# Second LayerNorm of three MLP chunks: turned rows kept and scaled instead of turned again

## The chip, the cores and the metric

The kernel runs on one core of a Trainium2 chip. A core has five engines that work side by side, each through its own list of instructions in order: PE (matrix products and transposes through the matrix unit, results into PSUM), ACT (functions of one input, element by element), DVE (element-wise work and reductions), POOL (element-wise work on SBUF) and SP (issues DMAs). They wait for each other through semaphores. The metric is the time of one execution on the device, in microseconds (us); lower is better.

## The reference

One block in which attention and an MLP run side by side on the same normalized input, for S = 2048 tokens of width D = 448, all in float32:

```python
xn = _layernorm(x, axis=-1)
out = x + A(xn) + B(xn)
# A: 16 heads of 28, one K and one V for all heads, softmax over 2048 keys
# B: y = _layernorm(xn); h = gelu(y @ w1 + b1)   (448 -> 1792);   h @ w2 + b2
```

The MLP normalizes a second time: `_layernorm(m) = (m - mean) / sqrt(var + 1e-5)` of rows that are already normalized. Their mean is zero but for rounding, so the second LayerNorm is one factor per token.

## The kernel before, in words

Tokens are handled in NCH = 4 chunks of CW = 512 (CT = 4 tiles of 128). A product in float32 is made of three products of two halves each: a high part and the rest, `xh` and `xl`, with the same split of the weights (`w1h`, `w1l`, `w2h`, `w2l`). For the products the normalized rows must stand turned, the 448 channels on partitions in four blocks b, the 512 tokens of a chunk along the row. The fourth block has 64 channels, which stand twice.

**Before the MLP** (lines 442 to 477). For each chunk four slots project Q, K and V from `xts[c, False]` (`q_slot`, line 352); beside them the next chunk is normalized and turned. That is `norm_parts` (line 249): `center` (line 255) scales and shifts a tile of 128 tokens on ACT and, for 64 channels, on DVE; `turn` (line 268) makes four transposes on PE into one PSUM bank, ACT copies the high part into `xh`, DVE subtracts it from the bank into `xl`. `xh` and `xl` are rings of two tiles. The evacuation of a Q slot writes `qe` and two stores of it to DRAM (`qd`, line 377); that of the first slot of a chunk also writes K: `kl` (line 372) and three copies into `ks` (line 374), all on SP's queue. SP also loads the weights here (lines 100 to 102 and 334), and POOL splits w1 (`w1_split`, line 325), whose buffers are then loaded again. The fourth group of slots turns chunk 0 for the second LayerNorm, with `lnq` and `lnqb` as factor and shift.

**The MLP** (lines 584 to 707) is 56 slots, chunk by chunk, 14 slots a chunk. PE's order is written out by hand: slot n runs `mlp1` of (c, ft), 11 matmuls into the one bank `ph`, and then `mlp2` of slot n - 2, 12 matmuls into four banks that gather over a chunk. Between them stand, nine to a slot, score tiles of the attention: L521 (a maximum over keys is reduced from it on DVE, L522) and L555 (kept, through DVE, and later exponentiated on ACT, L573, and stored to `td` by SP, L576). Both use the pool `mp`, three banks named m. ACT reads `ph` twice (`hx` L603, `hz` L604); POOL works out the inside of the GELU (L605, L606), ACT the tanh (L609), POOL the rest (L610, L611); in the next slot ACT makes `hh` (L616) and POOL `hl` (L618), which `mlp2` reads one slot later. `mlp2` has twelve places, `stages` 0 to 11, behind whose matmuls these pieces are issued. In chunk 0 each odd slot also splits a part of w2 (L342 on ACT, L346 on DVE and POOL).

The second LayerNorm of chunks 1 to 3 stands in slots 5, 7, 9, 11 and 13 of the chunk before (line 677): `norm_gen` (line 303) gets x again, four line loads of 224 KB (`line`, line 245), centers a tile at stage 8 and turns the one before at stage 4, through the bank `ph`. In these slots `texp` (the exps) stands at stages 5 and 6 rather than 0 and 1.

**After the MLP** come the scores, the exps and the products with V for all heads; they read what the earlier stages left in SBUF and DRAM, and are not touched.

SP, like every engine, issues in the order of the program. A DMA waits there for what it reads, for its buffer, and for the one eight DMAs earlier.

Of the kernel before, what the change touches and what calls it, by code (L numbers as in the profile page):

```python
# [19 lines left out]
CT = 4  # L20
# [11 lines left out]
RAWS = 2  # L32
GELU = 0.044715, 0.7978845608028654
LEAD = 11
NH = 8
HD = D // 2

# [2 lines left out]
def block_kernel(ctx, tc, x, wq, wk, wv, wo, w1, b1, w2, b2, out):  # L40
# [8 lines left out]
    mpx = ExitStack()  # L49
    mp = mpx.enter_context(tc.tile_pool(name="mp", bufs=3, space=PSUM))  # L50
    dram = ctx.enter_context(tc.tile_pool(name="dram", bufs=1, space=bass.MemoryType.DRAM))
    xt_p = ctx.enter_context(tc.tile_pool(name="xt", bufs=2))
    qmp = ctx.enter_context(tc.tile_pool(name="qmp", bufs=1))

    def heads_of(u):
# [5 lines left out]
    ld = dram.tile([4, CW], F32, name="ld")  # L61
    ad = dram.tile([P, NT, D], F32, name="ad")
    td = {u: dram.tile([32, 4, 4 * CT, 512], F32, name=f"td{u}") for u in TURNED}
    qd = [dram.tile([D, S], F32, name=f"qd{i}") for i in range(2)]

    ks = keep.tile([P, S], F32R, name="ks")
# [1 line left out]
    ident = keep.tile([P, P], F32, name="ident")  # L68

    ph1 = ExitStack()  # L70
    xl_p = ph1.enter_context(tc.tile_pool(name="xl", bufs=2))
# [5 lines left out]
    lnqb = wp.tile([P, NT], F32, name="lnqb")  # L77
    b1t = wp.tile([P, NF], F32, name="b1t")
    b1s = wp.tile([P, NF], F32, name="b1s")
    b2b = wp.tile([P, D], F32, name="b2b")  # L80
# [52 lines left out]
    make_identity(nc, ident)  # L133
    one = keep.tile([P, 1], F32, name="one")
    warm = keep.tile([P, 1], F32, name="warm")
    pool.memset(one, 1.0)
    pool.memset(f(wah[:, :, 0:64]), 0.0)
    pool.memset(f(wal[:, :, 0:64]), 0.0)
# [92 lines left out]
    def norm_both():  # L231
        dve.tensor_mul(lnq, lnp[:, :, 1], lnr)
        dve.tensor_mul(lnq, lnq, lnr)
        r = rstd(lnq, lnq, NT)
        next(r)
        yield
        next(r)
        dve.tensor_mul(lnq, lnq, lnr)
        dve.scalar_tensor_tensor(lnqb, lnp[:, :, 0], -1.0, lnq, op0=ALU.mult, op1=ALU.mult)
        act.activation(warm, one, AF.Tanh)  # L240
        yield
# [3 lines left out]
    def line(t):  # L245
        lines[t] = keep.tile([P, D], F32, name="a", bufs=4)
        nc.sync.dma_start(lines[t], xv[:, t, :])

    def norm_parts(c, second, first=False, bank=mtile):
        xh = xt_p.tile([P, 4, CW], F32R, name="xh")  # L250
        xl = xl_p.tile([P, 4, CW], F32R, name="xl")
        xts[c, second] = xh, xl
        xns = {}

        def center(k):
            t = CT * c + k
            if first:
                xn = f(wqp.tile([P, 2, CW], F32R, name="qe", bufs=5))[:, 0, :]
            else:
                xn = tmp.tile([P, 4 * P], F32, name="xn", bufs=2)  # L260
            scale, bias = (lnq, lnqb) if second else (lnr, lnb)
            src = lines.pop(t) if second and c else xin[t]
# [3 lines left out]
            xns[k] = xn  # L266

        def turn(k):
            sl = slice(k * P, (k + 1) * P)
            pt = bank([P, 4, P])  # L270
            for b in range(4):
                pe.transpose(pt[:, b, :], xns[k][:, b * P:(b + 1) * P], ident)
            act.activation(xh[:, :, sl], pt, AF.Copy)
            dve.tensor_sub(xl[:, :, sl], pt, f(xh[:, :, sl]))

        return center, turn
# [23 lines left out]
        turn(3)  # L300
        next(first)

    def norm_gen(c, bank):
        center, turn = norm_parts(c, True, False, bank)
        for k in range(CT + 1):
            if k > 0:
                turn(k - 1)
            yield
            if k < CT:
                center(k)  # L310
            yield

    wl_q = []

# [131 lines left out]
    for c in range(NCH):  # L446
        center, turn = norm_parts((c + 1) % NCH, c + 1 == NCH, bank=lambda shape: (qbank, mtile)[next(turns) % 2](shape))
        for i in range(4):
            ev = q_slot(c, i)
            if vt is not None:  # L450
                v_slot(c, vt)
                vt = None
            if evac is not None:
                vt = evac()
            evac = ev
            if i in ((2, 3) if c == 0 else (1, 3)):
                n = 2 * c + i // 3
                w1_split(n)
                if n < 2:
                    w1_load(n + 4)  # L460
                elif n == 3:
                    w1_load2(6)
                elif n in (4, 5):
                    w2_load(n - 4)
                if n in (2, 3):
                    qms.append(load_m(*heads[n - 2]))
                elif n in (4, 5):
                    load_m(TURNED[n - 4], 3, q3[n - 4])
            for job in more.get((c, i, True), ()):
                job()  # L470
            for part, k in (("", "c0 c1", "t0 c2 t1 c3", "t2 t3") if c == 0 else
                            ("c0 c1", "t0 c2 t1 c3", "t2 t3", ""))[i].split():
                (center if part == "c" else turn)(int(k))
            for job in more.get((c, i, False), ()):
                job()
    evac()
# [2 lines left out]
    def load_q(u, blocks=range(4)):  # L479
        c, g = units[u]  # L480
        cols = slice(c * CW, (c + 1) * CW)
        if u < 2 and 0 in blocks:
            qst.append(xt_p.tile([P, 4, CW], F32R, name="xh"))
# [138 lines left out]
    def mlp2(c, ft, stages):  # L622
        if ft == 0:
            m2s[c] = [m2p.tile([P, CW], F32, name=f"m2_{k}")[:, 0:D] for k in range(CT)]
        m2 = m2s[c]
        hh, hl = hs.pop((c, ft))
        terms = ((hh, w2h), (hh, w2l), (hl, w2h))
        order = [(k, i) for k in range(CT) for i in range(3)]
        if (c, ft) == (0, 0):
            order.sort(key=lambda e: e[1])  # L630
        for n, (k, i) in enumerate(order):
            h, w = terms[i]
            pe.matmul(m2[k], h[:, k * P:(k + 1) * P], w[:, ft, :], start=(ft == 0 and i == 0),  # L633
                      stop=(ft == NF - 1 and i == 2))
            if ft == NF - 1 and i == 2:
                t = CT * c + k
                a = lines.pop(t)
                dve.tensor_add(a, a, m2[k])
                nc.sync.dma_start(ad[:, t, :], a)
            stages[n]()  # L640
            yield

    def slot(n):
        nonlocal maxed, ending, later_low
        middle = high = low = none
        closing, ending = ending, none
        if n < len(mslots):
            if split(*mslots[n]):
                high, low = w2_split(n // 2)
                if n > 1:  # L650
                    high()
            middle, ending = yield from mlp1(*mslots[n])
# [16 lines left out]
    def none():  # L669
        pass  # L670

    norms, maxed, ending, later_low = {}, 0, none, none
    mslots = [(c, ft) for c in range(NCH) for ft in range(NF)]
    for c in range(1, NCH):
        g = norm_gen(c, lambda shape: php.tile(shape, F32, name="ph"))
        for i in range(CT + 1):
            norms[NF * (c - 1) + 5 + 2 * i] = lambda g=g: next(g, None)
    mxs.add(max_stream())
    done = 0
    for n in range(len(mslots) + 2):  # L680
        c, ft = mslots[n] if n < len(mslots) else (NCH, n - len(mslots))
        if 3 <= ft < 11 and ft % 2 and c < NCH - 1:
            line(CT * (c + 1) + (ft - 3) // 2)
        if 9 < ft:
            line(CT * c + ft - 10)
            if ft > 10:
                a = lines[CT * c + ft - 11]
                pool.tensor_add(a, a, b2b)
        if ft == 0 and n:
            a = lines[CT * c - 1]  # L690
            pool.tensor_add(a, a, b2b)
        if (c, ft) == (NCH - 1, 8):
            load_q(0)
# [260 lines left out]
```

## Time and profile before

| | us |
|---|---|
| median of 3 runs | 1092.79 |
| lowest and highest | 1092.52, 1094.23 |
| the profiled execution | 1092.67 |
| its span on the core | 1090.9 |
| PE, DVE, ACT, POOL busy in it | 1079.5, 910.4, 736.4, 562.5 |

The granted clock of PE was 0.999 over the span. In a row of the timeline stand the start, the time taken, the engine, the line, the operation and its tiles (`out<-in`), and in brackets the engine's idle time before it and what ended that. A row of a line's answer has the lowest, median and highest duration in ns, and the first and last start. The rows of the stretches have the busy time of each engine, the granted clock, the share of time in which the 16 DMA engines were busy, and GB/s. PEld is PE's load of weights, SPq an issue on SP's queue.

### The profile page before, as it was taken

Reading aid. Unit: us, or ns where it says so; the run is one execution under the profiler, and the core shown is the slowest. Engines: PE = TensorE matmul, PEld = TensorE weight load, DVE = VectorE, ACT = ScalarE, POOL = GpSimd, SP = SyncE. Lnnn points to the kernel's source line nnn. Section 1 sums busy time; section 2 is a strip of 40 time slices with the busy share of each in tenths; the row PEclk is TensorE's granted clock in tenths of the full one; section 3 lists DMA queues with packets and bytes.
Section 4 is the critical chain, followed back from the end, with each engine's and each line's share of the span. In section 5 each row is a group of like instructions: output and inputs, shape, how many; then the busy total and the mean of one; then the engine's idle time right before and its main releaser. Section 6 shows DMA issues by size and latency. Waiting matters only on the chain.

```text
span 1090.9 us, 17542 instructions
## 1 busy us (share of the span) xinstructions
PE 1079.5 (99%) x5777; PEld 713.7 (65%) x5777; DVE 910.4 (83%) x1847; ACT 736.4 (68%) x1279; POOL 562.5 (52%) x694
## 2 busy tenths in 40 slices
PE   9999999999999999999999999999999999999998
PEld 8778888888888888865555556555556455555444
DVE  7789889888988998887898997899986889876744
ACT  6675565666666666559777776677775777765783
POOL 6359787778767877854343433433342343243220
PEclk9999999999999999999999999999999999999999
DMA  8774555777877777767977799588797778895720
GB/s 274 214 231 136 154 145 157 194 176 185 217 181 180 183 201 180 214 161 156 200 189 175 183 212 214 141 198 193 183 202 183 175 172 194 203 197 137 183 46 35
DMA packets 140512, 195.15 MB, mean 179 GB/s; under 512 B 17086, under 2 KB 96116, under 8 KB 140420
## 3 DMA queue, kind: packets, MB, share of 16 engines
q1 hardware_dynamic: 127684, 172.11, 63.0%
q0 software_dynamic: 11328, 21.33, 8.9%
q8 instruction: 46, 0.75, 0.3%
q10 hardware_dynamic: 1408, 0.57, 0.2%
q14 instruction: 46, 0.38, 0.1%
HBM read 115.22 MB, written 77.71 MB: 177 GB/s over the span
## 4 chain that ended last, share of the span: by engine, by line
PE 89%; ACT 3%; DVE 3%; DMA 2%; POOL 1%; issue 1%; SPq 0%; DVEq 0%; ACTq 0%; POOLq 0%
PE po L840 22%; PE m L521 17%; PE m L871 17%; PE m L633 10%; PE ph L180 9%; PE m L555 5%; PE qp L180 1%; DMA td<-raw 1%; PE m L752 1%; DVE mx L522 1%; PE m L753 1%; PE m L754 1%; PE ph L185 1%; PE ph L183 1%; ACT raw L573 1%; PE m L399 1%
## 5 line engine op out<-in xcount | busy, mean ns | idle before, releaser
L522 DVE TENSOR_REDUCE mx<-m 128x1 f32<-128x512 f32 x784 | 506.5, 680 | 81.1 <-PE m L521 72.3
L872 ACT ACTIVATE p<-m 128x512 f32<-128x512 f32 x784 | 402.6, 609 | 163.2 <-PE m L871 163.2
L521 PE MATMUL m<-ks,qm 128*128 128x512 f32 x784 | 322.1, 411 | 0.1
L871 PE MATMUL m<-xh,ks 128*128 128x512 f32 x784 | 258.6, 399 | 1.0 <-DVE half L723 1.0
L840 PE MATMUL po<-p,vs 128*32 128x512 f32 x2048 | 246.0, 598 | 0.0
L521 PEld LDWEIGHTS m<-ks,qm 128*128 128x128 f32 x784 | 147.0, 187 | 117.9 <-ACT p L872 34.5
L871 PEld LDWEIGHTS m<-xh,ks 128*128 128x128 f32 x784 | 144.2, 188 | 52.0 <-ACT p L872 15.0
L556 DVE TENSOR_SCALAR_CACHE_REDUCE raw<-m 128x512 f32<-128x512 f32 x240 | 161.1, 689 | 15.2 <-PE m L555 7.0
L854 DVE STREAM_TRANSPOSE p<-half 128x1024 f32<-128x1024 f32 x120 | 148.2, 1236 | 5.3 <-PE po L840 3.3
L573 ACT ACTIVATE raw<-raw,m 128x1024 f32<-128x1024 f32 x120 | 133.1, 1151 | 0.0
L840 PEld LDWEIGHTS po<-p,vs 128*32 128x32 f32 x2048 | 53.5, 109 | 120.1 <-issue 114.2
L603 ACT ACTIVATE hx<-ph,b1t 128x512 f32<-128x512 f32 x55 | 37.9, 690 | 131.9 <-PE ph L185 122.1
L555 PE MATMUL m<-ks,q 128*128 128x512 f32 x240 | 94.8, 395 | 1.1 <-DVE mx L522 0.6
L618 POOL TENSOR_TENSOR hl<-hx,hh 128x512 fp32r<-128x512 f32 x56 | 73.2, 1306 | 34.6 <-ACT hh L616 34.6
L633 PE MATMUL m<-w2h,hl 128*128 128x448 f32 x224 | 82.5, 370 | 0.3 <-POOL hl L618 0.3
L633 PE MATMUL m<-w2l,hh 128*128 128x448 f32 x224 | 81.4, 365 | 0.4 <-DVE w2l L346 0.4
L633 PE MATMUL m<-w2h,hh 128*128 128x448 f32 x224 | 81.4, 364 | 0.1
L611 POOL TENSOR_TENSOR hx<-hx,hz 128x512 f32<-128x512 f32 x56 | 73.1, 1306 | 4.7
L606 POOL TENSOR_TENSOR hz<-hz,hx 128x512 f32<-128x512 f32 x56 | 72.8, 1299 | 4.7
L508 POOL DMA_DIRECT2D xh<-mn x15 | 8.1, 543 | 124.3 <-ACT mn L504 124.3
L180 PE MATMUL ph<-xh,w1h 128*128 128x512 f32 x165 | 65.0, 394 | 0.0
L180 PE MATMUL ph<-xh,w1l 128*128 128x512 f32 x165 | 64.6, 391 | 0.0
(181 smaller groups left out, 1376.0 us busy)
## 6 DMA issues: line engine op xcount, KB each, us to landing
td<-raw SPq DMA_DIRECT2D x240, 256.0 KB
half<-td SPq DMA_DIRECT2D x120, 512.0 KB
xh<-qd POOLq DMA_DIRECT2D x60, 168.0 KB, 4.6
a<-in_A_x_dram SPq DMA_DIRECT2D x32, 224.0 KB
qm<-qd POOLq DMA_DIRECT2D x112, 56.0 KB, 4.4
qd<-qe SPq DMA_DIRECT2D x24, 256.0 KB
qm<-qd SPq DMA_DIRECT2D x84, 56.0 KB
ad<-a SPq DMA_DIRECT2D x16, 224.0 KB
```

What stands on the lines that cost most here:

```text
L180: pe.matmul(ps, w, v, start=(n == 0), stop=False)
L521: pe.matmul(pm, qm[:, t * P:(t + 1) * P], ks[:, n * CW:(n + 1) * CW], start=True, stop=True)
L522: dve.tensor_reduce(mx[:, CT * j + t, n:n + 1], pm, axis=AX.X, op=ALU.max)
L555: pe.matmul(sc, q3[i][:, t * P:(t + 1) * P], ks[:, n * CW:(n + 1) * CW], start=True, stop=True)
L556: dve.tensor_scalar(raw[:, :, 4 * n:4 * n + 4, :].rearrange("p r b i -> p b r i"), sc.rearrange("p (b r i) -> p b r i", r=4, i=32), SCALE, ...
L573: act.activation(raw[:, rs], raw[:, rs], AF.Exp, bias=m3[:, 4:5], scale=1.0)
L618: pool.tensor_sub(hl, hx, f(hh))
L633: pe.matmul(m2[k], h[:, k * P:(k + 1) * P], w[:, ft, :], start=(ft == 0 and i == 0), stop=(ft == NF - 1 and i == 2))
L840: pe.matmul(po[32 * j:32 * j + 32, :], vs[:, kt, :], ps.pop((u, kt, j)), start=(kt == 0), stop=(kt == NT - 1))
L854: dve.transpose(p.rearrange("p k (g j) -> p g k j", j=32), halves[u, kt // 8][:, :, 32 * (kt % 8):32 * (kt % 8) + 64].rearrange("p g (k j) ...
L871: pe.matmul(s, ks[:, kt * P:(kt + 1) * P], qss[u][:, j, :], start=True, stop=True)
L872: act.activation(p, s, AF.Exp, scale=SCALE)
```

## The change

Chunks 1, 2 and 3 are no longer turned a second time. The rows that were turned for the projections are kept, and multiplied by the second LayerNorm's factor per token (`lna`, which is now kept apart from `lnq`).

- The factors of all tokens are turned once (`scale_rows`, one transpose, a store of 8 KB to `sd`), and for each chunk loaded as a row that stands on all partitions (`scale_load`, 256 KB).
- Chunk 3 stays where it is, in `xh1` and `xl1`. Chunks 1 and 2 are joined again in the projection stage: behind the first two centerings in the first slot of that chunk POOL adds `xh` and `xl` block by block (`join_all`, into the tiles `hx` and `hz` that the MLP uses later), and SP stores the four blocks to `xd1` or `xd2` behind the third and fourth slot of the chunk.
- In the MLP the order of the chunks is 0, 3, 1, 2. In slots 4, 6, 8 and 10 of the chunk before, one block b is begun: for chunks 1 and 2 SP loads it at the start of the slot (`take`), for chunk 3 DVE joins it at stage 6; POOL multiplies it at stage 11. At the start of the next slot ACT copies the high part into `xh`, and at stage 0 DVE subtracts to get `xl` (`scaled`).
- The exps are back at stages 0 and 1 in these slots; 12 line loads go. The rings `xh`, `xl` and `xn` become single tiles with names of their own. Chunk 0 is turned as before.

```diff
+MLP_ORDER = 0, 3, 1, 2
...
-    xt_p = ctx.enter_context(tc.tile_pool(name="xt", bufs=2))
+    xt_p = ctx.enter_context(tc.tile_pool(name="xt", bufs=1))
...
+    xd = {c: dram.tile([P, 4, CW], F32, name=f"xd{c}") for c in (1, 2)}
+    sd = dram.tile([NCH, CW], F32, name="sd")
...
-        r = rstd(lnq, lnq, NT)
+        r = rstd(lna, lnq, NT)
...
-        dve.tensor_mul(lnq, lnq, lnr)
+        dve.tensor_mul(lnq, lna, lnr)
...
+    def x_tiles(i):
+        return xt_p.tile([P, 4, CW], F32R, name=f"xh{i}"), xl_p.tile([P, 4, CW], F32R, name=f"xl{i}")
+
     def norm_parts(c, second, first=False, bank=mtile):
-        xh = xt_p.tile([P, 4, CW], F32R, name="xh")
-        xl = xl_p.tile([P, 4, CW], F32R, name="xl")
-        xts[c, second] = xh, xl
+        xh, xl = xts[c, second] = x_tiles(0 if second else c % 2)
...
-                xn = tmp.tile([P, 4 * P], F32, name="xn", bufs=2)
+                xn = part_tile() if k % 2 else wqp.tile([P, CW], F32, name="xn", bufs=1)
...
-    def norm_gen(c, bank):
-        center, turn = norm_parts(c, True, False, bank)
...
+    def part_tile():
+        return tmp.tile([P, CW], F32, name="part", bufs=1)
+
+    def scale_rows():
+        pa = mtile([NT, P])
+        pe.transpose(pa, lna, ident)
+        at = part_tile()[0:NT, 0:P]
+        dve.tensor_copy(at, pa)
+        nc.sync.dma_start(sd.rearrange("c (k p) -> (c k) p", p=P), at)
+
+    def scale_load(c):
+        scales[c] = tmp.tile([P, CW], F32, name="ab", bufs=1)
+        nc.sync.dma_start(scales[c], sd[c:c + 1, :].to_broadcast([P, CW]))
+
+    def join(c, b, eng, part):
+        xh, xl = xts[c, False]
+        eng.tensor_add(part, f(xh[:, b, :]), f(xl[:, b, :]))
+        return part
+
+    def join_all(c, xn):
+        pool.tensor_copy(gate, xn[:, 0:1])
+        for b in range(4):
+            n = P if b < 3 else 64
+            part = join(c, b, pool, hrp.tile([P, CW], F32, name="hx" if b < 2 else "hz", bufs=2))
+            later(c, 2 + b // 2, lambda n=n, b=b, part=part: nc.sync.dma_start(xd[c][0:n, b, :], part[0:n]))
+
+    def take(c, b):
+        n = P if b < 3 else 64
+        parts[c, b] = part_tile()
+        for r in range(0, P, n):
+            nc.sync.dma_start(parts[c, b][r:r + n], xd[c][0:n, b, :])
+
+    def scaled(c, b):
+        if c == 3:
+            parts[c, b] = join(c, b, dve, part_tile())
+        yield
+        pool.tensor_mul(parts[c, b], parts[c, b], scales[c])
+        yield
+        if b == 0:
+            xts[c, True] = xts[c, False] if c == 3 else x_tiles(c - 1)
+        yh, yl = xts[c, True]
+        act.activation(yh[:, b, :], parts[c, b], AF.Copy)
+        yield
+        dve.tensor_sub(yl[:, b, :], parts[c, b], f(yh[:, b, :]))
+        yield
...
+    later(3, 3, scale_rows)
...
+            if i == 0 and 0 < c < NCH - 1:
+                join_all(c, xn)
...
-        yh, yl = xts[c, True]
+        yh, yl = xts[MLP_ORDER[c], True]
...
+        work = seconds.pop(n, {})
+        work.get(-1, none)()
...
-        if n in norms:
-            stages = {4: norms[n], 5: texp, 6: texp, 7: closing, 8: norms[n], 9: middle, 10: low}
+        if 0 in work:
+            texp0 = stages.pop(0)
+            stages[0] = lambda: (work[0](), texp0())
+        stages.update((k, work[k]) for k in (6, 11) if k in work)
...
+    for i, c in enumerate(MLP_ORDER[1:]):
+        for b in range(4):
+            n = NF * i + 4 + 2 * b
+            g = scaled(c, b)
+            seconds[n] = {6: lambda g=g: next(g), 11: lambda g=g: next(g)}
+            seconds[n + 1] = {-1: lambda g=g: next(g), 0: lambda g=g: next(g)}
...
-        if 3 <= ft < 11 and ft % 2 and c < NCH - 1:
-            line(CT * (c + 1) + (ft - 3) // 2)
+        if ft == 1 and c < NCH - 1:
+            scale_load(MLP_ORDER[c + 1])
+        if 4 <= ft < 12 and ft % 2 == 0 and c < NCH - 1 and MLP_ORDER[c + 1] < 3:
+            take(MLP_ORDER[c + 1], ft // 2 - 2)
```

More of the change, by code (lines that the diff above doesn't have):

```diff
@@ L70, in block_kernel @@
     ph1 = ExitStack()
-    xl_p = ph1.enter_context(tc.tile_pool(name="xl", bufs=2))
+    xl_p = ph1.enter_context(tc.tile_pool(name="xl", bufs=1))
     wp = ph1.enter_context(tc.tile_pool(name="wp", bufs=1))
@@ L77, in block_kernel @@
     lnqb = wp.tile([P, NT], F32, name="lnqb")
+    lna = wp.tile([P, NT], F32, name="lna")
     b1t = wp.tile([P, NF], F32, name="b1t")
@@ L135, in block_kernel @@
     warm = keep.tile([P, 1], F32, name="warm")
+    gate = keep.tile([P, 1], F32, name="gate")
     pool.memset(one, 1.0)
@@ L259, in center @@
             else:
-                xn = tmp.tile([P, 4 * P], F32, name="xn", bufs=2)
+                xn = part_tile() if k % 2 else wqp.tile([P, CW], F32, name="xn", bufs=1)
             scale, bias = (lnq, lnqb) if second else (lnr, lnb)
-            src = lines.pop(t) if second and c else xin[t]
+            src = xin[t]
             act.activation(xn[:, 0:D], src, AF.Identity, bias=bias[:, t:t + 1], scale=scale[:, t:t + 1])
@@ L266, in center @@
             xns[k] = xn
+            return xn
         def turn(k):
@@ L301, in norm_first @@
         next(first)
-    def norm_gen(c, bank):
-        center, turn = norm_parts(c, True, False, bank)
[L305 to L311, printed above, removed]
+    scales, parts = {}, {}
+    def part_tile():
[37 more added lines that the diff above has]
+        yield
     wl_q = []
@@ L472, in block_kernel @@
                             ("c0 c1", "t0 c2 t1 c3", "t2 t3", ""))[i].split():
-                (center if part == "c" else turn)(int(k))
+                xn = (center if part == "c" else turn)(int(k))
+            if i == 0 and 0 < c < NCH - 1:
+                join_all(c, xn)
             for job in more.get((c, i, False), ()):
@@ L482, in load_q @@
         if u < 2 and 0 in blocks:
-            qst.append(xt_p.tile([P, 4, CW], F32R, name="xh"))
+            qst.append(xt_p.tile([P, 4, CW], F32R, name=f"xh{u}"))
             pool.memset(f(qst[u]), 0.0)
@@ L635, in mlp2 @@
             if ft == NF - 1 and i == 2:
-                t = CT * c + k
+                t = CT * MLP_ORDER[c] + k
                 a = lines.pop(t)
@@ L670, in none @@
         pass
-    norms, maxed, ending, later_low = {}, 0, none, none
+    maxed, ending, later_low = 0, none, none
     mslots = [(c, ft) for c in range(NCH) for ft in range(NF)]
[L674 to L677, printed above, removed]
+    seconds = {}
+    for i, c in enumerate(MLP_ORDER[1:]):
[4 more added lines that the diff above has]
+            seconds[n + 1] = {-1: lambda g=g: next(g), 0: lambda g=g: next(g)}
     mxs.add(max_stream())
@@ L681, in block_kernel @@
         c, ft = mslots[n] if n < len(mslots) else (NCH, n - len(mslots))
-        if 3 <= ft < 11 and ft % 2 and c < NCH - 1:
-            line(CT * (c + 1) + (ft - 3) // 2)
+        if ft == 1 and c < NCH - 1:
+            scale_load(MLP_ORDER[c + 1])
+        if 4 <= ft < 12 and ft % 2 == 0 and c < NCH - 1 and MLP_ORDER[c + 1] < 3:
+            take(MLP_ORDER[c + 1], ft // 2 - 2)
         if 9 < ft:
-            line(CT * c + ft - 10)
+            line(CT * MLP_ORDER[c] + ft - 10)
             if ft > 10:
-                a = lines[CT * c + ft - 11]
+                a = lines[CT * MLP_ORDER[c] + ft - 11]
                 pool.tensor_add(a, a, b2b)
         if ft == 0 and n:
-            a = lines[CT * c - 1]
+            a = lines[CT * MLP_ORDER[c - 1] + CT - 1]
             pool.tensor_add(a, a, b2b)
```

## The prediction

> **What bounds the kernel now.** I read the page first (shares, then the chain of waits), then the timeline of single slots of the MLP stage, then SP's queue ahead of that stage.
>
> ```profile
> span 1090.9 us, 17542 instructions
> PE 1079.5 (99%) x5777; PEld 713.7 (65%) x5777; DVE 910.4 (83%) x1847; ACT 736.4 (68%) x1279; POOL 562.5 (52%) x694
> ...
> PE 89%; ACT 3%; DVE 3%; DMA 2%; POOL 1%; issue 1%; SPq 0%; DVEq 0%; ACTq 0%; POOLq 0%
> ```
>
> PE is at work nearly without a hole and the chain runs over it. So whatever PE issues less shortens the run, and whatever holds PE up lengthens it. The second LayerNorm's turning is work of PE in the MLP stage:
>
> ```profile
> L272 PE MATMUL ph<-ident,xn x48: 272/273/330, 115.5 to 363.8; 128*128 128x128 f32 x48
> ...
> 93.05 0.69 ACT L603 ACTIVATE hx<-ph,b1t 128x512 f32<-128x512 f32 x1 [2.37 <-POOL hz L610]
> 167.23 0.69 ACT L603 ACTIVATE hx<-ph,b1t 128x512 f32<-128x512 f32 x1 [3.62 <-PE ph L185]
> 195.63 0.69 ACT L603 ACTIVATE hx<-ph,b1t 128x512 f32<-128x512 f32 x1 [2.65 <-PE ph L185]
> 268.61 0.69 ACT L603 ACTIVATE hx<-ph,b1t 128x512 f32<-128x512 f32 x1 [1.92 <-PE ph L185]
> 297.01 0.69 ACT L603 ACTIVATE hx<-ph,b1t 128x512 f32<-128x512 f32 x1 [2.65 <-PE ph L185]
> 304.05 0.69 ACT L603 ACTIVATE hx<-ph,b1t 128x512 f32<-128x512 f32 x1 [2.65 <-PE ph L185]
> 311.08 0.69 ACT L603 ACTIVATE hx<-ph,b1t 128x512 f32<-128x512 f32 x1 [2.00 <-PE ph L185]
> 369.75 0.69 ACT L603 ACTIVATE hx<-ph,b1t 128x512 f32<-128x512 f32 x1 [1.92 <-PE ph L185]
> ```
>
> There is one hx per slot, so their distance is PE's pace: 7.03 us for a plain slot (304.05 to 311.08). The three stretches with turns hold ten slots each and took 74.18, 72.98 and 72.74 us; less 70.3 that is 3.9, 2.7 and 2.4: **9.0 us is all that the turns cost today**, and all that can be won in this stage.
>
> **The change, part by part: the scaling chain.** What is put in their place is four steps per quarter of a chunk, on three engines in order: POOL multiplies (end of an even slot), ACT copies (ahead of the next slot's hx), DVE subtracts (after that slot's four L555 tiles and L562). Here is a plain pair of slots; PE begins the even one at 293.31 and so the odd one at 300.34 and the next at 307.37:
>
> ```profile
> 293.31 0.40 PE L180 MATMUL ph<-xh,w1h 128*128 128x512 f32 x1
> ...
> 300.25 0.62 ACT L616 ACTIVATE hh<-hx 128x512 fp32r<-128x512 f32 x1
> ...
> 302.93 1.29 POOL L611 TENSOR_TENSOR hx<-hx,hz 128x512 f32<-128x512 f32 x1
> 305.40 0.63 POOL L605 TENSOR_SCALAR hz<-hz 128x512 f32<-128x512 f32 x1 [1.18 <-ACT hz L604]
> 306.11 1.30 POOL L606 TENSOR_TENSOR hz<-hz,hx 128x512 f32<-128x512 f32 x1
> ...
> 304.27 0.16 DVE L562 TENSOR_REDUCE m<-m 128x1 f32<-128x4 f32 x1
> ...
> 303.99 0.40 PE L521 MATMUL m<-ks,qm 128*128 128x512 f32 x1
> ...
> 306.11 0.40 PE L521 MATMUL m<-ks,qm 128*128 128x512 f32 x1
> ...
> L522 DVE TENSOR_REDUCE mx<-m 128x1 f32<-128x512 f32 x784 | 506.5, 680 | 81.1 <-PE m L521 72.3
> ...
> 318.49 1.33 DVE L522 TENSOR_REDUCE mx<-m 128x1 f32<-128x512 f32 x2
> 320.76 0.69 DVE L274 TENSOR_TENSOR xl<-ph,xh 128x512 fp32r<-128x512 f32 x1 [0.94 <-ACT xh L273]
> 321.37 1.28 DVE L522 TENSOR_REDUCE mx<-m 128x1 f32<-128x512 f32 x2
> ```
>
> POOL's last step of the even slot (L611) ends at 304.22. The new multiply is of L606's kind, 1.30: 304.30 to 305.60; POOL's hole of 1.18 nearly takes it. But ACT meets the copy (0.62, as L616) ahead of hx, and hx started at 304.05. ACT now waits for POOL until about 305.66, copies to 306.28, and hx, hz, two exps and hh, all queued behind, go 2.1 us later. PE gets the one ph bank back when hx and hz have read it, some 1.3 us by hx's 0.69: 307.5, against its next slot at 307.37; that alone costs 0.1. POOL (L605, L618) and SP (the td stores) wait with ACT, and are on time again by the next even slot, since hl is read only there.
>
> DVE is held longer. It reaches its subtraction at 304.43, waits until the copy ends (306.28, 306.34 with the signal), and is free 0.61 after its start (320.76 to 321.37 above): 306.95 instead of 304.43. Queued behind it are the score tiles' maxima. The pool mp has three banks, so the fourth L521 (306.11) needs the first one's maximum, now 306.95 + 0.68 = 307.63 where it was 304.43 + 0.68 = 305.11: of the 2.5 us, 0.95 are covered, and PE stands until 307.7, **1.6 us**. The fifth then finds its bank free, and the next even slot starts late enough for POOL to be on time again, so each pair pays the same. The turn held DVE 0.94 + 0.61 = 1.55, which those 0.95 and PE's own 0.6 of transposes just covered. In the two chunks through DRAM: 8 pairs x 1.6 = 12.8, against 2.7 + 2.4 = 5.1 removed: **+7.7**. From below the bound is nothing held, -5.1; from above, with each slice also landing late by one multiply, 8 x 1.3 = 10.4 more.
>
> ```profile
> L346 DVE TENSOR_TENSOR w2l<-raw,w2h x7: 619/1034/1484, 78.8 to 164.0; 128x448 fp32r<-128x448 f32 x7
> ...
> L638 DVE TENSOR_TENSOR a<-a,m x12: 610/611/615, 175.2 to 381.7; 128x448 f32<-128x448 f32 x12
> ```
>
> The chunk in place (the second one) has the same chain, and DVE adds its halves first. Its odd slots also split w2: L346 follows the subtraction by one maximum, so the second maximum is 0.6 to 1.0 later and the fifth L521 waits as well: 2.0 to 2.4 a pair, taken 2.2. 4 x 2.2 = 8.8 against 3.9 removed: **+4.9**. The four joins are two-operand work from SBUF like L346, which takes 0.62 to 1.48 where L638, one operand from PSUM, takes 0.61 throughout; I take 1.0 each, which the 0.95 of the banks cover in an even slot. The Trainium skill (SBUF — State Buffer, "Who interferes with whom") says a DVE instruction with two SBUF inputs and a GpSimd one that reads SBUF shut each other out for a whole instruction. The spread of L346 agrees; by the full lock each join could wait a whole 1.30, and PE would lose up to 3 us more over the four than by the row's median, 1114 in the sum.
>
> **The change ahead of the MLP.** POOL adds eight joins (L606's 1.30 each), four a chunk, and SP eight stores of them (six of 256 KB, two of 128 KB), between the stores of q and ks:
>
> ```profile
> 40.00:60.00 20.00, 19.49 (x98) 15.32 (x97) 14.03 (x41) 14.93 (x27) 6.58 (x7) 1.00 0.80 233
> ...
> 55.26 1.75 SPq L438 DMA_DIRECT2D q<-qd  x4
> 57.11 2.19 SPq L377 DMA_DIRECT2D qd<-qe  x4
> 59.40 0.56 SPq L334 DMA_DIRECT2D raw<-in_B_w_dram  x1
> 60.01 2.91 SPq L438 DMA_DIRECT2D q<-qd  x4
> 63.02 0.82 SPq L377 DMA_DIRECT2D qd<-qe  x2
> 63.93 2.37 SPq L374 DMA_DIRECT2D ks<-kl  x2
> 66.39 0.75 SPq L374 DMA_DIRECT2D ks<-ks  x1
> ...
> 60.82 0.69 DVE L372 TENSOR_TENSOR kl<-qp,ks 28x512 fp32r<-28x512 f32 x1
> ...
> 68.74 0.19 PEld L183 LDWEIGHTS ph<-xh,w1h 128*128 128x128 f32 x1
> 68.96 0.19 PEld L185 LDWEIGHTS ph<-xl,w1h 128*128 128x128 f32 x1
> 69.29 0.19 PEld L555 LDWEIGHTS m<-ks,q 128*128 128x128 f32 x1
> ```
>
> SP issues without a pause, and late: kl was ready at 61.51 and its copy into ks left at 63.93. The last ks copy left at 66.39; the first MLP slot's fourth L555 needs it, and its load started at 69.29, 0.33 after the one in front where the pace is 0.22. There is no slack left, so what SP is late, PE stands. Eight issues of 0.41 (L377's 0.82 for two) and a little between them are 3.6 us; 1.83 MB at 291 GB/s (233 over its share 0.80) are 6.3. The third join of the second pair also waits for a store of the first, and holds POOL's w1 split, on which SP's w2 load waits. The DMA share here is nearer to full than to idle: I take **+6**, from 3 to 9, and no less than 0.
>
> **Edits at nothing.** 28 line loads become 16, and ten takes and three loads of scales come in: 13 for 12 on SP, under PE's slots, at like bytes. xh0/xh1, lna, and xn in two single buffers keep the old rotation and order. scale_rows is one transpose, one small copy and 8 KB, some 0.3 us, hidden while PE waits for ks; without that cover it costs 0.3. Exps that stood in later stages of the turning slots come earlier. The chunk order renames the residual's rows and moves nothing else. ACT loses the 12 centerings, off the path. The takes wait for the former subtraction, a slot and more back; POOL's multiply waits for the take, and behind it stand L605 and hl. A line load for the slot of 300.34 left at 303.63 and one for the slot two later, at 314.41, at 320.77:
>
> ```profile
> 303.63 1.07 SPq L247 DMA_DIRECT2D a<-in_A_x_dram  x1
> ...
> 320.77 0.37 SPq L247 DMA_DIRECT2D a<-in_A_x_dram  x1
> ```
>
> These are 3.3 and 6.4 us into their slots; with 3 us to land (66.39 to 69.29) that makes 6 to 9.5, and the multiply starts 11 in. So they are hidden, by 1.5 us at worst.
>
> **Sum.** The profiled execution took 1092.67 us (span 1090.9), 0.1 under the median of the runs. 1092.67 + 7.7 + 4.9 + 6 = 1111.3: **1111 us**.
>
> **The rivals.**
> - *Only the MLP slots pay.* The stores hide, as SP catches up or the ks copies aren't late: 1092.67 + 12.6 = 1105. For it: before 57 us the DMA share is 0.80, not full. Against: SP's unbroken issue.
> - *All hidden, faster.* The mechanism is DVE's subtraction: if the copy ends no more than 0.35 us after DVE gets there (0.95 less the 0.61 of the subtraction), by 304.8 in these rows, PE never stands and sheds its 48 transposes; with the stores hidden too, 1092.67 - 9.0 = 1084. For it: PE's 99% and POOL's hole of 1.18. Against: ACT's place ahead of hx, 1.6 us before POOL is done.
> - *The slots gain, the stores cost.* 1092.67 - 9.0 + 6 = 1090; on either side of no change.
> - *Late takes.* If slices land behind four td stores and the q loads, past 11 us into the slot, POOL, ACT, DVE and PE all wait: 1 to 2 us in each of 8 pairs: 1119 to 1127.
>
> **How the numbers follow.** Forecast 0.47 (own range 1105 to 1118), only the slots 0.17, all hidden 0.10, gain against stores 0.12, late takes 0.14. A measurement tells about 0.2%, 2.2 us. Faster: 0.10 and most of the 0.12, 0.17; same 0.05; slower 0.78. The range 1088 to 1122 leaves out "all hidden" and the upper half of the late takes, 0.17.
>
> **What would show it.** In the profile after: ACT's copy waiting on POOL some 3 us once per pair and hx moved 2 us; DVE's subtraction waiting some 1.9 on ACT; PE's weight loads waiting on DVE's maxima, 1.6 a pair, so pairs of about 15.7 us where turning pairs took 14.7 (14.06 + 5.1 / 8); the ks copies some 6 us later and PE idle as long in the first slot. Pairs of 14.06 and a first slot without a hole would make the forecast wrong.

## The result, and the profile after

| | us |
|---|---|
| before, median | 1092.87 |
| after, median | 1112.29 |
| ratio, 95% interval | 1.0168, 1.0157 to 1.0179 |
| the profiled execution after, its span | 1112.99, 1111.2 |

One of the six executions after took 1312.08 us at a granted clock of 0.752, where the other five show 0.997 to 0.999; their median is 1111.62, and the ratio is of them alone. So the change makes the kernel 18.8 us slower, where 18.3 were predicted (1111). The page of the kernel after, against the shares and the chain shown of before:

```profile
span 1111.2 us, 17484 instructions
PE 1082.6 (97%) x5730; PEld 709.5 (64%) x5730; DVE 917.9 (83%) x1840; ACT 728.4 (66%) x1267; POOL 584.3 (53%) x716
...
PE 80%; DVE 6%; ACT 6%; POOL 5%; issue 2%; DMA 1%; SPq 0%; ACTq 0%; POOLq 0%; DVEq 0%
```

PE's share fell from 99% to 97%. In the chain of waits it gave up 9 points, which DVE, ACT and POOL took: there is now a path that runs through the three steps of the scaling. Where the time went is read from the first matmul of a slot at six places: the first two MLP slots, the first slot of each later chunk, and the last slot of all. Before:

```profile
66.24 0.39 PE L180 MATMUL ph<-xh,w1h 128*128 128x512 f32 x1
...
69.66 0.39 PE L180 MATMUL m<-xh,w1h 128*128 128x512 f32 x1
...
163.54 0.39 PE L180 MATMUL ph<-xh,w1h 128*128 128x512 f32 x1
...
264.92 0.39 PE L180 MATMUL ph<-xh,w1h 128*128 128x512 f32 x1
...
366.05 0.39 PE L180 MATMUL ph<-xh,w1h 128*128 128x512 f32 x1
...
458.61 0.40 PE L180 MATMUL ph<-xh,w1h 128*128 128x512 f32 x1
```

And after:

```profile
71.23 0.48 PE L185 MATMUL ph<-xh,w1h 128*128 128x512 f32 x1
...
76.53 0.39 PE L185 MATMUL m<-xh,w1h 128*128 128x512 f32 x1
...
174.53 0.40 PE L185 MATMUL ph<-xh,w1h 128*128 128x512 f32 x1
...
280.13 0.40 PE L185 MATMUL ph<-xh,w1h 128*128 128x512 f32 x1
...
385.88 0.40 PE L185 MATMUL ph<-xh,w1h 128*128 128x512 f32 x1
...
479.32 0.40 PE L185 MATMUL ph<-xh,w1h 128*128 128x512 f32 x1
```

The differences are 5.0 ahead of the MLP, 1.9 in its first slot, 4.1 in the rest of the first chunk, 4.2 and 4.6 in the second and third, and 0.9 in the last, which scales nothing: 20.7. From there to the end the new kernel is 0.4 faster, which leaves the 20.3 between the two profiled executions (the one after, 1112.99, is the slowest of the five).

**The pairs.** The waits of DVE, ACT and PE's weight loads between 90 and 480 us (total, times, longest), and one pair of the third chunk:

```profile
DVE xl L355 <- ACT xh L353: 19.6, 12, 1.8
...
ACT xh L353 <- POOL part L348: 49.4, 12, 4.2
...
PEld m L569 <- DVE mx L570: 21.9, 20, 1.9
```

```profile
312.51 0.69 ACT L651 ACTIVATE hx<-ph,b1t 128x512 f32<-128x512 f32 x1 [2.72 <-PE ph L190]
...
319.66 1.29 POOL L348 TENSOR_TENSOR part<-part,ab 128x512 f32<-128x512 f32 x1
...
320.99 0.63 ACT L353 ACTIVATE xh<-part 128x512 fp32r<-128x512 f32 x1 [4.10 <-POOL part L348]
321.52 0.67 ACT L651 ACTIVATE hx<-ph,b1t 128x512 f32<-128x512 f32 x1
321.65 0.69 DVE L355 TENSOR_TENSOR xl<-part,xh 128x512 fp32r<-128x512 f32 x1 [1.69 <-ACT xh L353]
...
323.00 0.19 PEld L569 LDWEIGHTS m<-ks,qm 128*128 128x128 f32 x1 [1.55 <-DVE mx L570]
...
328.13 0.69 ACT L651 ACTIVATE hx<-ph,b1t 128x512 f32<-128x512 f32 x1 [2.24 <-PE ph L190]
```

Read from the top: POOL multiplies, ACT stood 4.10 us for it, DVE stood 1.69 for ACT, and the weight load of a score tile stood 1.55 for a maximum. That is the predicted chain; the waits of ACT and DVE stand twelve times, once in each pair. From the first to the last `hx` are 15.62 us where two plain slots take 14.20.

**Ahead of the MLP.** DVE, POOL and SP in the projection stage after, in order of time:

```profile
35.14 2.50 POOL L328 TENSOR_TENSOR hz<-xh,xl 128x512 f32<-128x512 f32 x2
...
36.26 1.44 DVE L270 TENSOR_SCALAR xn<-a,lnr,lnb 128x64 f32<-128x64 f32 x1
...
53.78 2.54 POOL L328 TENSOR_TENSOR hz<-xh,xl 128x512 f32<-128x512 f32 x2 [2.66 <-DMA xd<-hz]
56.29 1.62 POOL L374 TENSOR_TENSOR w1l<-raw,w1h 128x672 fp32r<-128x672 f32 x1
...
56.39 1.56 DVE L238 TENSOR_TENSOR lnq<-lnq,lnr 128x16 f32<-128x16 f32 x1
...
71.71 1.66 SPq L419 DMA_DIRECT2D ks<-kl  x2
73.47 0.75 SPq L419 DMA_DIRECT2D ks<-ks  x1
```

The ks copies leave 7.8 and 7.1 us later than before (63.93, 66.39), where some 6 were forecast. But PE does not stand for them that long. DVE's 64-wide centering takes 1.44 us beside POOL's joins, where the same line takes 0.31 as a rule, and a multiplication of 16 columns takes 1.56 beside POOL's w1 split, where its kind takes 0.17. So the projection itself is late, and nothing in the prediction said that: `kl`, which the ks copies read, is ready at 66.43, where it was ready at 61.51. The kernel before shows the sign of it, one small step of the same sequence on DVE (most of its neighbours of 16 columns take 0.17 or 0.18) beside a w1 split that POOL began at 52.99 and that took 1.64:

```profile
53.03 1.63 DVE L195 TENSOR_SCALAR rs<-lnq 128x16 f32<-128x16 f32 x1
```

### The profile page after: what moved, and what is told of

Its sections match the earlier page's. It is cut to its first block, busy times and chain, and to the rows that moved or that the text cites. A ratio compares the mean times of both kernels' runs of the same rounds, so it can differ in the third digit from the quotient of the medians.

```text
span 1111.2 us, 17484 instructions
## 1 busy us (share of the span) xinstructions
PE 1082.6 (97%) x5730; PEld 709.5 (64%) x5730; DVE 917.9 (83%) x1840; ACT 728.4 (66%) x1267; POOL 584.3 (53%) x716
## 4 chain that ended last, share of the span: by engine, by line
PE 80%; DVE 6%; ACT 6%; POOL 5%; issue 2%; DMA 1%; SPq 0%; ACTq 0%; POOLq 0%; DVEq 0%
PE po L897 21%; PE m L928 17%; PE m L569 16%; PE ph L185 8%; PE m L681 7%; PE m L603 4%; ACT raw L621 2%; POOL hl L666 1%; POOL part L348 1%; DVE mx L570 1%; PE m L809 1%; POOL hx L659 1%; PE m L810 1%; PE m L811 1%; PE ph L190 1%
## 5 line engine op out<-in xcount | busy, mean ns | idle before, releaser
L604 DVE TENSOR_SCALAR_CACHE_REDUCE raw<-m 128x512 f32<-128x512 f32 x240 | 163.6, 690 | 20.7 <-PE m L603 13.7
L185 PE MATMUL ph<-xl,w1h 128*128 128x512 f32 x165 | 65.4, 397 | 0.0
```

The lines of the kernel that those rows point to most:

```text
L185: pe.matmul(ps, w, v, start=(n == 0), stop=False)
L604: dve.tensor_scalar(raw[:, :, 4 * n:4 * n + 4, :].rearrange("p r b i -> p b r i"), sc.rearrange("p (b r i) -> p b r i", r=4, i=32), SCALE, ...
```

## The experiments

Three questions: what PE waits for in a pair; what makes the 6.9 us ahead of the second MLP slot; and why plain slots take 7.10 us after, where they took 7.03.

**Only the subtraction late.**

```diff
-        stages.update((k, work[k]) for k in (6, 11) if k in work)
+        stages.update((k, work[k]) for k in (6, 7, 10, 11) if k in work)
...
-            seconds[n + 1] = {-1: lambda g=g: next(g), 0: lambda g=g: next(g)}
+            seconds[n + 1] = {-1: lambda g=g: next(g), 10: lambda g=g: next(g)}
```

> Only DVE's subtraction is moved, from stage 0 of the odd slot to stage 10; ACT's copy stays ahead of hx. Theory of the prediction (DVE, held at the subtraction, is late with the maxima, and PE stands for a bank): the odd slots of the twelve pairs fall from 8.5 to 9.1 us to a plain slot's 7.1, 8 x 1.44 + 4 x 1.9 = 19 us in all, 1112.3 - 19 = 1093 us, and the weight loads' wait on the maxima (21.9 us in 90 to 480) goes. Rival (ACT's copy, which waits 3 to 4 us for POOL ahead of hx, keeps the bank ph occupied, and that is what PE stands for): the pairs stay as they are, 1110 to 1113 us, with PE's waits on ACT in place of those on DVE.

Measured: 1104.52 us, ratio 1.011 (1.0095 to 1.0125): some 7 of the 19 us came back. In the chunks through DRAM seven of eight odd slots take 7.1 to 7.7 us where they took 8.5 to 8.9; the eighth kept 8.87. A pair of the second chunk, and POOL's multiply ahead of the eighth:

```profile
215.80 0.63 ACT L353 ACTIVATE xh<-part 128x512 fp32r<-128x512 f32 x1 [4.10 <-POOL part L348]
216.33 0.67 ACT L651 ACTIVATE hx<-ph,b1t 128x512 f32<-128x512 f32 x1
...
217.51 0.68 DVE L355 TENSOR_TENSOR xl<-part,xh 128x512 fp32r<-128x512 f32 x1
...
359.55 1.28 POOL L348 TENSOR_TENSOR part<-part,ab 128x512 f32<-128x512 f32 x1 [1.76 <-DMA part<-xd]
```

ACT still waits 4.10 for POOL and `hx` is as late as in the kernel after, DVE waits for no copy, and PE does not stand. So ACT's order alone costs PE nothing there. It does in the eighth slot: a take landed late, POOL waited 1.76 for it and ACT 5.71 for POOL, and the next slot's first weight load stood 2.00 for the bank `ph`, which ACT had not yet read. The chunk in place did not gain:

```profile
141.47 0.63 DVE L391 TENSOR_TENSOR w2l<-raw,w2h 128x448 fp32r<-128x448 f32 x1 [1.48 <-ACT w2h L387]
```

There DVE now waits for the w2 copy, which stands on ACT behind the copy that waits for POOL; and in this run the joins take 1.45 to 1.81 and the subtractions 1.41, against 1.0 and 0.6 in the prediction. Its odd slots stay at 8.5 to 8.7 and the even ones rise to 7.7.

**Copy and subtraction both late**, at stages 7 and 10.

```diff
+            seconds[n + 1] = {7: lambda g=g: next(g), 10: lambda g=g: next(g)}
```

> Copy and subtraction both late: stages 7 and 10 of the odd slot. Theory of the prediction: within 1.5 us of the run with the subtraction alone moved, 1092 to 1093, since ACT's order ahead of hx was worth 0.1 us a pair. Rival (ACT's order): this run alone gains, 1093 here against 1110 to 1113 there. If each holds PE in part, the two runs lie between, and their difference is ACT's part. With the joins and stores ahead of the MLP unchanged, the first MLP slot still starts near 71.2 us of the span, and its wait for ks stays.

Measured: 1113.1 us, ratio 1.0185 (1.017 to 1.02). Neither theory forecast this. The hold has moved into the next even slot, which takes 8.2 us (8.8 in chunk 0; behind the last pair of a chunk 9.2, in chunk 0 11.3):

```profile
218.75 0.62 ACT L353 ACTIVATE xh<-part 128x512 fp32r<-128x512 f32 x1
...
219.48 0.77 DVE L355 TENSOR_TENSOR xl<-part,xh 128x512 fp32r<-128x512 f32 x1 [1.83 <-ACT xh L353]
...
220.90 0.19 PEld L603 LDWEIGHTS m<-ks,q 128*128 128x128 f32 x1 [1.27 <-DVE mx L570]
```

At stage 7 the copy has the exps, `hh` and the tanh in front of it, ends later than DVE reaches stage 10, and DVE waits 1.83 again. It is the same mechanism in another place: what counts is whether DVE meets its subtraction before the copy is done.

**Only the copy behind hx and hz**, the subtraction where it was. (This run also has the small new tiles elsewhere, a change of its own that is described below.)

```diff
+            seconds[n + 1] = {0: lambda g=g: (next(g), next(g))}
```

> The changed kernel with the tiles put back, and ACT's copy moved behind hx and hz (stage 0) while DVE's subtraction stays at stage 0: the mirror of the run that moved only the subtraction. Theory of the prediction (DVE's hold is what PE stands for): the copy still ends with POOL's multiply, so DVE is held as long, the pairs stay at 15.5 us in the two chunks through DRAM, and the time at about 1110; only hx starts on time again, and chunk 0's w2 split gains some 0.5 a pair. Rival (ACT's order matters by itself): pairs of 14.1 to 14.5, 1095 to 1100.

Measured: 1120.79 us, ratio 1.0254 (1.024 to 1.0269), pairs of 16.7 us. The mirror of the first run: `hx` is on time and the kernel is slower still.

```profile
218.57 1.27 POOL L654 TENSOR_TENSOR hz<-hz,hx 128x512 f32<-128x512 f32 x1
...
218.58 1.80 DVE L355 TENSOR_TENSOR xl<-part,xh 128x512 fp32r<-128x512 f32 x1 [1.75 <-ACT xh L353]
...
221.03 0.19 PEld L569 LDWEIGHTS m<-ks,qm 128*128 128x128 f32 x1 [2.73 <-DVE mx L570]
```

DVE waits as long as ever, 1.75, and then its subtraction takes 1.80 instead of 0.69: POOL's next product, no longer late with `hx`, starts in the same moment and runs 1.27. DVE's hold is 1.2 us longer, and PE's wait grows from 1.55 to 2.73. Chunk 0 did not gain either; its odd slots take 9.1 to 9.6.

**Joins on DVE, stores as they were.**

```diff
-        pool.tensor_copy(gate, xn[:, 0:1])
...
-            part = join(c, b, pool, hrp.tile([P, CW], F32, name="hx" if b < 2 else "hz", bufs=2))
+            if c == 2 and b > 1:
+                part = join(c, b, dve, f(hrp.tile([P, CW], F32R, name=("hh", "hl")[b - 2])))
+            else:
+                part = join(c, b, dve, hrp.tile([P, CW], F32, name="hx" if b < 2 else "hz", bufs=2))
```

> The eight joins ahead of the MLP run on DVE instead of POOL, at the same place, and two of chunk 2 write other buffers, so that none waits for a store of chunk 1; the stores stay. Theory A (POOL's joins shut DVE's 64-wide centerings out, 1.44 and 1.04 us instead of 0.31, and the joins that wait for a store push POOL's w1 split onto DVE's small steps, 1.56 and 1.46 instead of 0.17): the first MLP slot starts 3 to 4 us earlier, at 67 to 68 us, and if SP's ks copies come earlier with it, 1108 us. Theory B, the prediction's (SP's queue is what is late, whoever joins): the projection gains, but the ks copies still leave at 71 to 73 us and PE waits for them in the first slot instead: 1111 to 1112.5.

Measured: 1112.98 us, ratio 1.018 (1.0163 to 1.0197). Both halves came true: the first MLP slot starts at 67.77 us instead of 71.23, and then takes 8.80 instead of 5.30, so the second starts at 76.57, as before the edit (76.53).

```profile
72.00 1.66 SPq L421 DMA_DIRECT2D ks<-kl  x2
...
76.01 0.77 PE L605 MATMUL m<-ks,q 128*128 128x512 f32 x1 [4.75 <-DMA ks<-ks]
```

The ks copies leave at 72.00, although the projection was 3.5 us earlier and `kl` was ready at 62.19: SP alone is late enough for the whole loss.

**Joins on POOL, no stores.**

```diff
-            later(c, 2 + b // 2, lambda n=n, b=b, part=part: nc.sync.dma_start(xd[c][0:n, b, :], part[0:n]))
...
-            nc.sync.dma_start(parts[c, b][r:r + n], xd[c][0:n, b, :])
+            nc.sync.dma_start(parts[c, b][r:r + n], qd[0][b * P:b * P + n, c * CW:(c + 1) * CW])
```

> The eight stores of the joined rows are left out, and the MLP's takes read rows of q of the same size instead (so the second LayerNorm of chunks 1 and 2 gets other data: the stores are the part left out); POOL's joins stay. Theory B, the prediction's (SP late by the stores): all of the 6.9 us ahead of the second MLP slot come back, 1105.5. Theory A (POOL's joins block DVE): 1.6 us at each of the two groups of joins stay, the rest, about 3.5, comes back: 1108.5 to 1109.

Measured: 1111.31 us, ratio 1.0169 (1.0154 to 1.0184). The first MLP slot starts at 70.95 (71.23), the second at 74.51 (76.53): only 2.0 come back. The centerings of both chunks are held now:

```profile
35.70 1.42 DVE L270 TENSOR_SCALAR xn<-a,lnr,lnb 128x64 f32<-128x64 f32 x1
...
50.85 1.42 DVE L270 TENSOR_SCALAR xn<-hl,lnr,lnb 128x64 f32<-128x64 f32 x1
```

So with POOL's joins alone the second slot is 4.9 us behind the kernel before, with SP's stores and the joins on DVE 6.9, as with both. They lie beside each other, and taking away one shows little. The Trainium skill (SBUF — State Buffer, "Who interferes with whom") says that a DVE `tensor_scalar` between SBUF tiles can take both port pairs, of which GpSimd shares one, and is shut out while a GpSimd instruction holds it; 1.42 against 0.31 us beside a join of 1.27 agrees.

**The small new tiles elsewhere.** `gate` (4 bytes a row) and `lna` (64) had moved all tiles of the MLP by 32 to 96 bytes a row.

```diff
-    lna = wp.tile([P, NT], F32, name="lna")
...
-    gate = keep.tile([P, 1], F32, name="gate")
...
     wal = wqp.tile([P, 3, CW], F32R, name="wal")
+    lna = wqp.tile([P, NT], F32, name="lna")
+    gate = wqp.tile([P, 1], F32, name="gate")
```

> As the changed kernel, with the two new small tiles (gate, 4 bytes a row, and lna, 64) put into another pool behind the tiles of the MLP, so that xh, xl, q3, qm, w1h, w1l, hh, hl and b2b lie at the addresses of the kernel before again (they had moved by 32 to 96 bytes a row). Theory C (the plain MLP slot takes 7.10 us in place of 7.03, even in the last chunk where nothing is scaled, because of where the operands lie): 7.03 again, 54 x 0.07 = 3.8 us less, 1108.5. Rival (the pace is the chip's or comes from the new chunk order): 7.10 stays, 1112.

Measured: 1110.46 us, ratio 1.0162 (1.0147 to 1.0177). The plain slots take 7.03 again, but the pairs' odd slots keep 8.5, since DVE sets their length; and its profiled execution has a stall of some 2 us in two slots near the end of the third chunk (9.7 and 8.0) that the kernel after lacks. In the time the gain is not told from none; in the slots it is. The second MLP slot starts at 75.48 instead of 76.53, so some of what is lost ahead of it may be the tiles' place too; but in this stage executions of the same instructions differ (75.48 here, 74.10 in the next run), so that a microsecond there proves little.

**Copy behind hx and hz, subtraction at stage 10**, on top of that.

```diff
-            seconds[n + 1] = {-1: lambda g=g: next(g), 0: lambda g=g: next(g)}
+            seconds[n + 1] = {0: lambda g=g: next(g), 10: lambda g=g: next(g)}
```

> The run before with ACT's copy put behind hx and hz (stage 0 of the odd slot) and DVE's subtraction at stage 10, so that neither meets a step that is not done. Theory of the prediction (PE stands only because DVE is held): pairs of two plain slots in the two chunks through DRAM, 8 x 1.44 less; in chunk 0 the w2 split no longer waits behind the copy, but the joins (1.8 us) and subtractions (1.4 us) of SBUF data remain, some 0.5 a pair, so 4 x 1.3 less: 1108.5 - 16.7 = 1092. Rival (a late subtraction makes a wait of its own, as with the copy at stage 7, where the next even slots took 8.2 to 8.8): 1100 to 1104.

Measured: 1090.98 us, ratio 0.9982 (0.9972 to 0.9993). The pairs through DRAM are two plain slots:

```profile
211.75 0.69 ACT L651 ACTIVATE hx<-ph,b1t 128x512 f32<-128x512 f32 x1 [1.84 <-PE ph L190]
218.79 0.69 ACT L651 ACTIVATE hx<-ph,b1t 128x512 f32<-128x512 f32 x1 [2.65 <-PE ph L190]
220.24 0.63 ACT L353 ACTIVATE xh<-part 128x512 fp32r<-128x512 f32 x1 [0.19 <-POOL part L348]
```

ACT now waits 0.19 for POOL here and 1.0 at most, and DVE waits for no copy anywhere in the stage. 19.5 us came back from moving two instructions; in chunk 0 some 0.2 a pair remains.

**DVE's joins, and the stores from POOL's or from ACT's queue**, on top of that; the joins as above, and `nc.scalar` in the second kernel.

```diff
-            later(c, 2 + b // 2, lambda n=n, b=b, part=part: nc.sync.dma_start(xd[c][0:n, b, :], part[0:n]))
+            later(c, 2 + b // 2, lambda n=n, b=b, part=part: nc.gpsimd.dma_start(xd[c][0:n, b, :], part[0:n]))
```

> The run before with the eight joins on DVE and their eight stores issued from POOL's queue instead of SP's. Theory (joins on POOL and stores on SP each cost nearly the same 5 to 7 us ahead of the second MLP slot, and hide each other, so that only both together bring it back): the first MLP slot starts at 66.5 to 67.8 and takes about 3.5, the second starts at 70 to 71 instead of 76.5: 6 us less than the run before, 1086. Rival (the DMA engines, not SP's issuing, are what is full: 1.8 MB more): the ks copies stay late and no more than 2 us come back, 1090.

> The same with the stores issued from ACT's queue. If issuing is all that mattered, 1086 as from POOL; if ACT, 14 of 20 us busy there and in the turns' path, loses some 0.4 us for each of eight issues, 3 us of it come back: 1089. If the DMA engines are full, 1090 for both queues.

Measured: 1087.78 (ratio 0.9956, 0.9941 to 0.9971) and 1087.43 us (0.9957, 0.994 to 0.9974). The second MLP slot starts at 72.55 and 71.47, against 74.10 in the run they build on and 69.66 in the kernel before. The medians gain 3.2 and 3.6 of the 6 that were expected. With some 2 us of uncertainty the times alone do not rule out the 2 that full DMA engines would have left; but the ks copies leave earlier, at 68.10 and 65.89 instead of 69.60, while as many bytes are moved. From POOL, PE still waits 1.9 for the ks copies; from ACT it does not, but ACT's queue is held 2.62 by one issue of two stores (at 39.54), and a later turn waits 1.3 for ACT's centering. So neither rival is the whole story: issuing mattered, and something of the 6 stays. The two are not told apart. The second is the fastest version by its median, 5.5 us under the kernel before, and is called so below.

**Four bytes, sixty-four bytes, and only the moving operand.** To the fastest version an unused tile is added in front of the MLP's tiles (one line, of 4 or of 64 bytes a row); the third run places small unused tiles so that `xh` and `xl` alone stand off.

```diff
+    gate = keep.tile([P, 1], F32, name="gate")
```

> The run with the stores on ACT's queue, with one tile of 4 bytes a row that nothing uses put back into the pool keep, which moves every tile of the MLP behind it by 32 bytes a row; not one instruction differs. Theory C (where the operands lie sets the pace): plain slots 7.10 again, 54 x 0.07 = 3.8 us more than 1087.4, so 1091.2. Rival (something else of the run with the tiles put back made 7.03): 7.03 and 1087.4.

> As the run with the unused tile of 4 bytes a row, with 64 bytes a row instead, so that the MLP's tiles move by 64 bytes. If 64 bytes are the unit that counts, plain slots take 7.03 and the time is 1087.4; if any move off the old place costs, or 128 is the unit, 7.10 and 1091.

> As the run with the stores on ACT's queue, with unused tiles placed so that only xh and xl, the moving operands of the first MLP product, start 32 bytes past a multiple of 64; w1, w2, hh, hl, q3 and qm start on a multiple of 64 as in the kernel before. If it is the moving operand's place that costs, 11 of a slot's 32 products pay, and a plain slot takes 7.04 to 7.08 us: 1088.5 to 1090.5. If it is the weights' (w1, hh, hl, q3, qm, whose loads alternate with the products), 7.01 to 7.03 and 1087.4 to 1087.8.

Measured: 1090.61 (0.9982, 0.9973 to 0.9991), 1087.84 (0.9953, 0.9939 to 0.9966) and 1089.49 us (0.9968, 0.9955 to 0.998). Two neighbouring plain slots of the last chunk, by their `hx`; without a tile:

```profile
399.49 0.69 ACT L653 ACTIVATE hx<-ph,b1t 128x512 f32<-128x512 f32 x1 [2.65 <-PE ph L190]
406.52 0.69 ACT L653 ACTIVATE hx<-ph,b1t 128x512 f32<-128x512 f32 x1 [2.65 <-PE ph L190]
```

With 4 bytes (all tiles 32 bytes further):

```profile
402.36 0.69 ACT L653 ACTIVATE hx<-ph,b1t 128x512 f32<-128x512 f32 x1 [2.70 <-PE ph L190]
409.44 0.69 ACT L653 ACTIVATE hx<-ph,b1t 128x512 f32<-128x512 f32 x1 [2.70 <-PE ph L190]
```

With `xh` and `xl` alone 32 bytes off:

```profile
401.43 0.69 ACT L656 ACTIVATE hx<-ph,b1t 128x512 f32<-128x512 f32 x1 [2.68 <-PE ph L193]
408.50 0.69 ACT L656 ACTIVATE hx<-ph,b1t 128x512 f32<-128x512 f32 x1 [2.69 <-PE ph L193]
```

With 64 bytes:

```profile
400.16 0.69 ACT L653 ACTIVATE hx<-ph,b1t 128x512 f32<-128x512 f32 x1 [2.63 <-PE ph L190]
407.17 0.69 ACT L653 ACTIVATE hx<-ph,b1t 128x512 f32<-128x512 f32 x1 [2.63 <-PE ph L190]
```

That is 7.03, 7.08, 7.07 and 7.01. An unused tile of 4 bytes costs some 3 us of the median, one of 64 nothing that can be told. For the tiles that PE reads in these slots, the third run and the one with 64 bytes differ in one thing that counts: `xh` and `xl` stand 32 bytes past a multiple of 64 in the third, all others on a multiple of 64 in both. So the place of the first product's moving operand makes some 0.05 of the 0.07 us that lie between the run with 64 bytes and that with 4.

## Why the prediction was right

The median of the five executions lies 0.6 us above the forecast, but the terms missed in both directions, so that much of this closeness is luck. The table goes by the profiled execution. The pairs are counted as odd slots less a plain 7.10.

| step | predicted | measured |
|---|---|---|
| pairs through DRAM, 8 | 12.8 - 5.1 = +7.7 | 12.1 - 5.1 = +7.0 |
| pairs in place, 4 | 8.8 - 3.9 = +4.9 | 7.2 - 3.9 = +3.3 |
| ahead of the MLP | +6 | 5.0 + 1.9 = +6.9 |
| pace of plain slots | 0 | +3.5, the rest |
| sum to the last slot | +18.6 | +20.7 |

- **The DVE hold: right, and shown.** The copy waited 4.10 (some 3 forecast), the subtraction 1.69 (1.9), PE 1.55 at the weight load and 1.44 by the slots (1.6). Three runs separate its causes: with DVE free and ACT late PE is free (but for the one late take), with `hx` on time and DVE held PE stands, and wherever the copy ends too late for DVE the stall returns. Its statement that ACT's order costs 0.1 a pair held in the chunks through DRAM.
- **The chunk in place: a join that was too cheap, a pair that was too dear.** A join in the kernel after:

```profile
118.44 1.66 DVE L328 TENSOR_TENSOR part<-xh,xl 128x512 f32<-128x512 f32 x1
```

The step "1.0 each" for the joins, taken from the median of L346, failed: they took 1.44, 1.66, 1.67 and 1.66. Yet PE lost nothing by it, as the even slots that hold them took 7.07 to 7.11. The pair cost 1.7 to 2.0, not 2.2: the split of w2 behind the subtraction (L346 before, L391 after) took 0.62 on DVE each time, the low end of the 0.6 to 1.0 that were counted.
- **The stores: right in size, wrong in place.** "PE idle as long in the first slot" failed. POOL's eight joins had been given a duration (1.30) and no effect on others. They held DVE's centerings, and the join that waits for a store, which the prediction named, pushed the w1 split onto DVE's small steps. That was a second cause of nearly the same size; since the two overlap, the sum did not show it.
- **Edits at nothing: failed for the tiles.** The new tiles were counted as names. They moved the operands by 32 to 96 bytes and added 0.07 us to every plain slot, some 3.5 us in all.
- **The rivals.** Late takes are not seen in the kernel after: no wait of POOL on a take. They are near, though: with only the subtraction late POOL waited 0.61 and 1.76 for two of them, and the second cost its slot 1.8 us. "All hidden" named as its deciding point a copy that ends no later than 0.35 us after DVE gets there. The run with the copy behind `hz` and the subtraction at stage 10 meets it, in another order, and PE sheds the turns and stands in no pair through DRAM; with the tiles put back and the stores off SP that is 1087.4, of the 1084 that the rival gave.

## What to carry to other kernels

When a chain of three engines is threaded through a full schedule, place each step where its input is already there: a step that must wait holds everything behind it on its engine, and with three PSUM banks in front of PE the cover was under a microsecond here (DVE was held 1.69 + 0.61 = 2.3 us in a pair through DRAM, and PE lost 1.44). When work is put on POOL, look at what DVE does with SBUF data in the same microseconds, and price the two together. And before an edit is costed at nothing, compare the addresses of the tiles that PE streams: a new tile of 4 bytes in front of them cost 3 us here.

## What the hardware showed that was not expected

- The place of a moving operand: with rows that start 32 bytes past a multiple of 64 a plain slot of 32 matmuls took 7.07 to 7.10 us, on a multiple of 64 it took 7.01 to 7.03. Whether the rest, 0.01 to 0.03, comes from the places of the other tiles was not separated, and what in the chip does it is open.
- POOL against DVE on tiny work: 16 columns took 1.56 us instead of 0.17, and 64 columns 1.44 instead of 0.31. Both ended within 0.1 us of POOL's instruction beside them (57.95 and 37.70, POOL 57.91 and 37.64), so what was lost went by POOL's duration and not by one's own.
- The same join of two 128x512 tiles takes some 0.64 us on DVE and 1.27 on POOL, and DVE had a hole of 2.3 us where POOL's first four joins had been put, nearly enough for them.
- Two causes of about 5 and 7 us that lie beside each other: removing one gave 0 and 2 us at the second MLP slot, and both moved together 3.2 to 3.6 of the median. Some 1.8 us ahead of the second MLP slot stays in the fastest version, and its cause is open.
